# Order of side work around an attention pipeline: weight lengths a block later, tanh ahead of a projection, and a last head that evicts before it normalises

## The chip, the cores and the metric

The kernel runs on one core of a Trainium2 chip. The metric is the device time of one execution in microseconds; of several runs the median counts.

## The reference

Two branches share a layer-normalised input of 2048 rows and 640 columns. One is attention over a key and value cache with 32 heads of 192 columns and 2048 keys, the other a gated feed-forward net with 1536 hidden columns. Everything comes in as bf16.

```python
xn = _layernorm(x)                                   # (1, 2048, 640)
q = (xn @ wq).reshape(1, 2048, 32, 192).transpose(0, 2, 1, 3)
scores = einsum("bhqd,bhkd->bhqk", q, k_cache) * 192 ** -0.5
o = einsum("bhqk,bhkd->bhqd", softmax(scores), v_cache)
s = o.transpose(0, 2, 1, 3).reshape(1, 2048, 6144) @ wo
h = silu(xn @ w1) * (xn @ w3)
g = silu(h @ w2)
return x + s * g
```

## The kernel before

The attention part is a software pipeline over heads `h` (0 to 31), query blocks `qb` of 512 rows (0 to 3), and steps `p` (0 to 7), each with 256 keys. In a step TensorE makes scores of 256 keys by 512 queries (`scores`, line 550), ScalarE takes their exponential into a weight tile (`weights`, line 558), and one and a half steps or so behind TensorE multiplies earlier weights with the values into two PSUM banks `obank0` and `obank1` (`values_quads`, line 629; `values`, line 609). After step 7 of a block the banks are evicted while the next block starts: for heads 2 to 30 ("quads") ScalarE copies one bank to `oa` and DVE adds the other into `ot` (`evict_quads`, lines 653 and 654); for heads 0, 1 and 31 DVE makes `osum` of each bank and divides it by its row sum (`evict`, lines 581 to 588). There is one pair of value banks, so TensorE's first value product of a block waits for the eviction of the block ahead. The score banks, `ps_st`, are two; the weight tiles, pool `pp`, are three, each for two steps.

In step 1 of each block TensorE also projects a block of the next head's queries (`project_chunk`, line 355), and DVE, ScalarE and POOL copy the result into `qA`, `qF`, `qS` and `qD` (lines 378 to 385). In the last head that place holds the last columns of the feed-forward branch (`hidden_last`, results `gl` and `ul`, lines 950 and 951). In the projection's spare columns a part of the feed-forward branch is carried: every odd head takes `tanh` of the part that came with the head ahead of it (`gate`, line 524, ScalarE) and multiplies twice on DVE (`product`, lines 529 and 531).

For quads heads the row sums of the weights are made on DVE by a tree of additions (`row_sums`, line 662: twice a block the sum of four weight tiles, `fours`, then `join`, `fold`, `ends`, which leaves `e`), a DMA transpose of `e` into `eT`, and `turned_sums` (lines 702 to 709), which adds up, inverts and normalises the evicted outputs into `ostage`.

The exponentials need a bound for each head. It is made from the largest keys (`fold_keys`, three DVE reductions, line 407, and three small POOL copies into `sh`) and from the lengths of the weight columns (`column_lengths`): a DMA transpose of the head's weights into `wt`, issued on the SP queue (line 421), two DVE instructions that square and add (`squares`, line 428), and seven small ones for the root (`roots`, lines 434 to 442). `head_bound` puts the two together and adds over partitions on POOL (line 502).

Where side work stands is set by hand. Nearly everything is pinned to program order, engine by engine (`pin`). A counter `clock` goes up by one a step. `chores` hold work with a due time: `later(2, fours)`, `later(4, ...)` for the rest of the tree, `later(6, turned_sums)`; `do_chores` runs all that are due at the end of each step. `lazy` is a list of bound work that is taken one piece a step, from its head, in steps 5, 6 and 7 of even heads and of head 1, and in step 5 of other odd heads; a piece is taken only if its due time has come. In an even head the lengths of head `h + 1` are asked for in block 0, step 3, and those of `h + 2` in block 2. All engines work through their instructions in order, so an instruction that waits keeps everything behind it.

The tail, after head 31, makes the rest of the feed-forward branch and the output product; the change does not touch it.

Of the kernel before, what the change touches and what calls it, by code (L numbers as in the profile page):

```python
# [30 lines left out]
def _kernel_impl(ctx, tc, A_x, A_k_cache, A_v_cache, A_wq, A_wo, B_w1, B_w3, B_w2, out):  # L31
    nc = tc.nc
    _, SQ, D = A_x.shape
    _, H, SK, dh = A_k_cache.shape
# [131 lines left out]
    with ExitStack() as actx:  # L166
# [236 lines left out]
        def fold_keys(h):  # L403
            hd = heads[h]

            def piece(j):
                pin(nc.vector.tensor_reduce(out=hd["mk"][:, j:j + 1], in_=hd["L"]["KT"][:, j, :], axis=AX.X, op=ALU.max,
                                            apply_absolute_value=True))
                if j == 2:
                    sh, up, down = shift_tile()  # L410
                    up(hd["mk"])
                    down(hd["mk"])
                    hd["mk"] = (hd["mk"], sh)

            hd["mk"] = stt.tile([P, 3], F32, tag="mk", name="mk")
            return [(0, piece, (j,)) for j in range(3)]

        def column_lengths(h):
            L = loads.get(h) or heads[h]["L"]
            wt = fdp.tile([P, 2 * DC, P], BF16, tag="wt", name="wt")  # L420
            pin(nc.sync.dma_start_transpose(out=wt[:], in_=L["wq"][:].rearrange("p s c -> p (s c)")))
            ss = stt.tile([P, 2], F32, tag="ss", name="ss")
            pin(nc.vector.memset(ss[:], 0.0))

            def squares(t):
                r0 = (0, PGW)[t]
                v = wt[r0:P, :, ROWS[t]]
                pin(nc.vector.scalar_tensor_tensor(out=v, in0=v, scalar=1.0, in1=v, op0=ALU.mult, op1=ALU.mult,  # L428
                                                   accum_out=ss[r0:P, t:t + 1]))

            def roots():
                y = stt.tile([P, 2], F32, tag="ly", name="ly")
                z = stt.tile([P, 2], F32, tag="lz", name="lz")
                pin(nc.vector.tensor_scalar(out=ss[:], in0=ss[:], scalar1=float(D), scalar2=None, op0=ALU.mult))
                pin(nc.vector.tensor_scalar(out=y[:].bitcast(I32), in0=ss[:].bitcast(I32), scalar1=1, scalar2=None,
                                            op0=ALU.logical_shift_right))
                pin(nc.vector.tensor_scalar(out=y[:].bitcast(I32), in0=y[:].bitcast(I32), scalar1=0x1FC00000, scalar2=None, op0=ALU.add))
                pin(nc.vector.reciprocal(out=z[:], in_=y[:]))
                pin(nc.vector.tensor_tensor(out=z[:], in0=z[:], in1=ss[:], op=ALU.mult))
                ln = stt.tile([P, 2], F32, tag="ln", name="ln")  # L440
                pin(nc.vector.scalar_tensor_tensor(out=ln[:], in0=z[:], scalar=1.0, in1=y[:], op0=ALU.mult, op1=ALU.add))
                pin(nc.vector.tensor_scalar(out=ln[:], in0=ln[:], scalar1=0.5, scalar2=None, op0=ALU.mult))
                L["ln"] = ln

            return [(clock[0] + 4, squares, (0,)), (clock[0] + 4, squares, (1,)), (clock[0] + 4, roots, ())]

        def head_bound(h):
            hd = heads[h]
# [2 lines left out]
        def shift_tile():  # L451
            sh = stt.tile([P, 2], F32, tag="sh", name="sh")
            keep = pin if 0 in heads else (lambda x: x)
            keep(nc.gpsimd.memset(sh[ROWS[0], 1:2], 0.0))

            def up(m):
                keep(nc.gpsimd.tensor_copy(out=sh[ROWS[0], 0:1], in_=m[ROWS[1], 1:2]))

            def down(m):
                keep(nc.gpsimd.tensor_copy(out=sh[ROWS[1], 0:1], in_=m[ROWS[0], 2:3]))  # L460
                keep(nc.gpsimd.tensor_copy(out=sh[ROWS[1], 1:2], in_=m[ROWS[0], 1:2]))
            return sh, up, down
# [195 lines left out]
        def later(wait, f, *a):  # L658
            chores.append((clock[0] + wait, f, a))
# [55 lines left out]
        clock = [0]  # L715
        chores = []
        lazy = []
        aq = {}

        def do_chores(h, qb, p):  # L720
            for c in [c for c in chores if c[0] <= clock[0]]:
                chores.remove(c)
                c[1](*c[2])
            slots = (5, 6, 7) if h % 2 == 0 or h == 1 else (5,)
            if p in slots and lazy and lazy[0][0] <= clock[0]:
                _, f, a = lazy.pop(0)
                f(*a)
# [236 lines left out]
        for h in range(1, H):  # L964
            if h >= H // 2 and ffn_w_loads:
                ffn_w_loads.pop(0)()
            if h == 1:
                loads[3] = load_weights(3)
                while loads[2]["rest"]:
                    loads[2]["rest"].pop(0)()  # L970
            elif h + 2 == H:
                load_last()
            if h + 1 < H:
                start_head(h + 1)
            hd = heads[h]
            hd.update(sums=dict(w=[], t=[]), ox={})
            if h == 1:
                lengths = [2]
                todo = []
            elif h + 1 < H:  # L980
                lengths = [] if h % 2 else [h + 1] + [h + 2] * (h + 2 < H)
                todo = [h + 1]
            else:
                lengths = todo = []
            chunks = [[0], [1], [2], [3]] if h + 1 < H else [[0, 1], [2, 3], [], []]
            gated = []
            for qb in range(NQB):
                post = []
                if (h, qb) == (H - 1, 2):
                    while chores:  # L990
                        clock[0] += 1
                        do_chores(h, qb, 2)
                    astack.close()
                    acc["hTp"] = fstack.enter_context(tc.tile_pool(name="hTp", bufs=2, side="right"))

                def extra():
                    if h % 2 == 1:
                        for c in chunks[qb]:
                            gate = swiglu_chunk(h // 2, heads[h - 1]["qF"], hd["qF"], c)
                            gated.append(gate if h + 1 < H else gate())  # L1000
                    quads = before["quads"] if qb == 0 else hd["quads"]
                    if h + 1 < H:
                        post.append(project_chunk(h + 1, qb, quads=quads, cast_low=nc.scalar.copy if hd["quads"] else None))
                    else:
                        post.append(hidden_last(qb, quads))

                for p in range(NPAIR):
                    step(hd, qb, p, extra if p == 1 else None)
                    if p == 4 and 1 < h < H - 2:
                        load_ahead(h + 2, qb)  # L1010
                    if p == 3 and (h, qb) != (1, 0):
                        for k in lengths[:1] if qb % 2 == 0 or h == 1 else []:
                            lazy.extend(column_lengths(k))
                            lengths = lengths[1:]
                        for k in todo or ([2] if (h, qb) == (1, 1) else []):
                            lazy.extend(fold_keys(k))
                            lazy.append((0, head_bound, (k,)))
                        todo = []
                    if (h, qb, p) == (1, 0, 7):
                        copy_keys(heads[2]["L"])  # L1020
                        loads[3].update(load_keys(3))
                    if (h, qb, p) == (1, 2, 7):
                        copy_keys(loads[3])
                    if h + 1 < H:
                        if p == 3 and gated:
                            f = gated.pop(0)
                            later(1, lambda f=f: gated.append(f()))
                            later(3, lambda: gated.pop(0)())
                    else:
                        if p > 4 and gated:  # L1030
                            gated.pop(0)()
                        if p == 3:
                            gated.append(post.pop()())
            while lazy:
                _, f, a = lazy.pop(0)
                f(*a)
                assert 0, "late"
            heads.pop(h - 1, None)
            before["quads"] = hd["quads"]
# [143 lines left out]
    with ExitStack() as dctx:  # L1183
# [32 lines left out]
        todo = [lambda qb=qb, j=j: parts.append(load_part(pools, qb, j)) for qb in range(LB) for j in range(4)][3:]  # L1216
# [177 lines left out]
```

## Time and profile before

| | |
|---|---|
| median of 3 runs | 1941.54 us (1940.84 to 1942.04) |
| profiled execution | 1942.01 us |
| span of that execution on the core | 1940.5 us |
| TensorE matmul busy | 1919.0 us (99%) |
| DVE busy | 1440.0 us (74%) |
| ScalarE busy | 1351.7 us (70%) |
| granted TensorE clock | 1.0 of full speed |

Times in a timeline are microseconds from the span's start. A row of a timeline gives start, length, engine, line, operation, written and read tiles, and in brackets how long the engine was idle just before and what ended that. PE is TensorE, ACT is ScalarE, SP is the queue that issues most DMAs. A matmul's end is modelled, so the idle time of PE is best read together with the pitch at which the same instruction comes again in each block.

### The profile page before, as it was taken

What the parts mean: (1) busy time and instruction counts of PE and PEld (TensorE: products, weight loads), DVE (VectorE), ACT (ScalarE), POOL (GpSimd) and SP (SyncE); (2) the same over time, 40 slices, a digit from 0 to 9 for tenths busy, and PEclk for the clock granted to TensorE, in tenths of its full rate; (3) what the DMA queues carried; (4) which work ended last, traced back from release to release, by engine and by line L of the source; (5) the groups of instructions that cost most, each with busy time, mean ns of one, the idle gap of its engine ahead of it and who ended that gap; (6) DMA issues with size and microseconds to landing.
All of it is one profiled execution on the core that took longest, in us unless ns stands there. A gap on an engine that the chain in (4) does not pass through costs nothing.

```text
span 1940.5 us, 75768 instructions
## 1 busy us (share of the span) xinstructions
PE 1919.0 (99%) x34608; PEld 1550.9 (80%) x34631; DVE 1440.0 (74%) x2326; ACT 1351.7 (70%) x1405; POOL 602.9 (31%) x757
## 2 busy tenths in 40 slices
PE   9999999999999999999999999999999999999999
PEld 5666698999989998989898989888988986454446
DVE  8569897888888888888888979897988875521111
ACT  7778888788878788888788888888787877210000
POOL 3423334333434333334323343334343320000000
PEclk9999999999999999999999999999999999999999
DMA  7724446444553455445544454436444523946763
GB/s 169 138 53 74 104 84 101 86 99 86 92 97 84 99 81 98 81 103 91 103 84 102 68 107 72 113 73 106 84 99 88 97 42 111 276 84 144 165 148 79
DMA packets 535684, 197.22 MB, mean 102 GB/s; under 512 B 486896, under 2 KB 528848, under 8 KB 535360
## 3 DMA queue, kind: packets, MB, share of 16 engines
q1 hardware_dynamic: 522416, 162.71, 43.3%
q0 software_dynamic: 8256, 24.58, 5.1%
q8 instruction: 271, 4.44, 1.0%
q10 hardware_dynamic: 4688, 5.05, 0.8%
q14 instruction: 53, 0.43, 0.1%
HBM read 54.26 MB, written 31.98 MB: 44 GB/s over the span
## 4 chain that ended last, share of the span: by engine, by line
PE 88%; DVE 7%; DMA 3%; issue 1%; ACT 1%; SPq 0%; POOL 0%; DVEq 0%; ACTq 0%
PE st L550 30%; PE obank L629 28%; PE ps L355 13%; PE ps_s L1138 8%; DVE tree L662 3%; PE obank L609 3%; PE ps_s L1094 3%; DMA wt<-wq 3%; PE ps_f L1158 2%; PE ps_gu L927 1%; PE ps_f L1174 1%; DVE ot L654 1%; DVE wt L428 1%; DVE e L662 1%; DVE qA L378 0%
## 5 line engine op out<-in xcount | busy, mean ns | idle before, releaser
L558 ACT ACTIVATE pT<-st,nb 128x1024 bf16<-128x1024 f32 x1016 | 1125.9, 1114 | 197.2 <-PE st L550 170.0
L629 PE MATMUL obank<-pT,vt 64*64 64x512 bf16 (+1 forms) x14848 | 846.3, 323 | 11.4 <-DVE ot L654 11.3
L629 PEld LDWEIGHTS <-vt 64*64 64x64 bf16 x14848 | 604.1, 107 | 89.0 <-issue 20.0
L550 PE MATMUL st<-qS,KM 64*64 64x512 bf16 (+1 forms) x1951 | 469.9, 376 | 0.2 <-DVE ul L951 0.2
L550 PE MATMUL st<-qD,KT 64*64 64x512 bf16 (+1 forms) x1951 | 470.1, 376 | 0.0
L550 PE MATMUL st<-qA,KT 64*64 64x512 bf16 (+1 forms) x1951 | 470.0, 376 | 0.0
L550 PEld LDWEIGHTS <-KT 64*64 64x64 bf16 (+1 forms) x7808 | 379.6, 106 | 54.3 <-issue 0.6
L550 PE MATMUL st<-qA,KM 64*64 64x512 bf16 (+1 forms) x1951 | 413.9, 376 | 0.0
L550 PE MATMUL st<-qS,KT 64*64 64x512 bf16 (+1 forms) x1951 | 413.8, 376 | 0.1
L550 PE MATMUL st<-qF,KT 64*64 64x512 bf16 (+1 forms) x1951 | 413.8, 376 | 0.0
L381 POOL COPY qS<-qA 64x512 bf16<-64x512 bf16 x256 | 292.4, 1142 | 79.7 <-DVE qA L378 45.4
L662 DVE TENSOR_TENSOR tree<-pT,pT 128x2048 bf16<-128x2048 bf16 x232 | 300.7, 1296 | 2.0 <-ACT pT L558 2.0
L355 PE MATMUL ps<-xnT,wq 64*64 64x512 bf16 (+1 forms) x2390 | 298.2, 376 | 0.0
L355 PE MATMUL ps<-xnS,wq 64*64 64x512 bf16 (+1 forms) x2390 | 290.6, 376 | 0.0
L662 DVE TENSOR_TENSOR tree<-tree 128x2048 bf16<-128x2048 bf16 x232 | 261.8, 1129 | 4.0
L355 PEld LDWEIGHTS <-wq 64*64 64x64 bf16 (+1 forms) x4780 | 220.8, 107 | 30.5
L550 PEld LDWEIGHTS <-KM 64*64 64x64 bf16 (+1 forms) x3904 | 196.5, 106 | 31.1 <-issue 4.5
L385 POOL COPY qD<-qF 64x512 bf16<-64x512 bf16 x127 | 95.4, 751 | 366.3 <-ACT qF L378 362.4
L1138 PE MATMUL ps_s<-oT,wo_sb 128*128 128x512 bf16 x705 | 154.9, 379 | 0.8
L378 DVE CAST qA<-ps 128x512 bf16<-128x512 f32 x120 | 82.9, 691 | 80.0 <-ACT qF L378 79.4
L1138 PEld LDWEIGHTS <-wo_sb 128*128 128x128 bf16 x720 | 70.4, 98 | 84.9 <-issue 0.2
L653 ACT COPY oa<-obank 128x768 f32<-128x768 f32 x116 | 92.8, 800 | 62.6 <-PE obank L629 62.6
(159 smaller groups left out, 1669.8 us busy)
## 6 DMA issues: line engine op xcount, KB each, us to landing
o_scr<-ostage SPq DMA_DIRECT2D x64, 384.0 KB, 2.9
vt<-in_A_v_cache_dram SPq DMA_DIRECT2D x62, 384.0 KB, 5.0
wo_sb<-in_A_wo_dram POOLq DMA_DIRECT2D x1, 7680.0 KB, 30.5
wq<-in_A_wq_dram POOLq DMA_DIRECT2D x31, 160.0 KB, 4.1
hT_scr<-hblk SPq DMA_DIRECT2D x16, 256.0 KB, 2.9
xnS<-xnT POOLq DMA_DIRECT2D x8, 320.0 KB, 6.1
wq<-in_B_w_dram POOLq DMA_DIRECT2D x31, 80.0 KB, 3.7
wq<-in_A_wq_dram POOLq DMA_DIRECT2D x31, 80.0 KB, 3.3
```

What stands on the lines that cost most here:

```text
L355: pin(nc.tensor.matmul(halves[t][c, :], lhsT=w[ROWS[t], s, c], rhs=xs[ROWS[t], s // 2, qs], start=(s == 0), stop=(s == 2 * DC - 1)))
L378: pin(c(out=dst[:, qs], in_=src))
L381: keep(nc.gpsimd.tensor_copy(out=qS[ROWS[t], qs], in_=qA[ROWS[1 - t], qs]))
L385: keep(copy(out=qD[:, qs], in_=qF[PGW:P, qs]))
L550: pin(nc.tensor.matmul(st2[c, t * 512:(t + 1) * 512], lhsT=k[:, c], rhs=q[ROWS[t], qs], start=(s == 0), stop=(s == 2)))
L558: pin(nc.scalar.activation(out=pT2, in_=st2[:], func=ACT.Exp, scale=SCALE, bias=nb[:]))
L609: pin(nc.tensor.matmul(acc["o"][b][:, r, (j % 2) * 256:(j % 2) * 256 + DH + 1], lhsT=pT2[ROWS[r], t * 512 + j * P:t * 512 + (j + 1) * P], ...
L629: pin(nc.tensor.matmul(acc["o"][r][ROWS[c], int(low), 0:n], lhsT=vt[ROWS[r], t, p, c0:c0 + DT], rhs=pT2[ROWS[r], t * 512 + q0:t * 512 + q0 ...
L653: pin(nc.scalar.copy(out=oa[:], in_=banks[0]))
L662: pin(nc.vector.tensor_tensor(out=out, in0=a, in1=b, op=ALU.add))
L1094: pin(nc.tensor.matmul(ps, lhsT=oT[:, k, :], rhs=wo_sb[:, k, c0:c1], start=(k == 0), stop=(k == OC - 1)))
L1138: pin(nc.tensor.matmul(ps_of[d], lhsT=wo_sb[:, k, d * P:(d + 1) * P], rhs=part(k // KQ)[:, k % KQ, :], start=(k == 0), stop=(k == OC - 1)))
```

## The change

Three edits.

First, the pieces of `column_lengths` fall due ten steps after their DMA is issued instead of four, and in `lazy` the three key maxima of a head go ahead of the length pieces, with `head_bound` behind both. Block 0 of an even head then has the three maxima in steps 5 to 7, block 1 the two squares and the roots, block 2 the bound; before, block 0 had one square, block 1 a square, the roots and a maximum, block 2 two maxima and the bound. The lengths of `h + 2`, in block 3, keep their steps.

Second, in every odd head that is not a quads head (head 1; the last head did so already) the `tanh` is issued in step 1, ahead of the projection, instead of in step 4. The multiplications stay in step 6.

Third, in the last head `do_chores` returns at once in steps 0 and 1 of a block. What is left over from head 30 (the last `fours`, two `turned_sums`, and the end of the tree) is then issued in step 2, behind the evictions and behind the copies `gl` and `ul`.

```diff
@@ column_lengths
-            return [(clock[0] + 4, squares, (0,)), (clock[0] + 4, squares, (1,)), (clock[0] + 4, roots, ())]
+            return [(clock[0] + 10, f, a) for f, a in ((squares, (0,)), (squares, (1,)), (roots, ()))]
@@ do_chores
         def do_chores(h, qb, p):
+            if h == H - 1 and p < 2:
+                return
             for c in [c for c in chores if c[0] <= clock[0]]:
@@ extra, in step 1
                             gate = swiglu_chunk(h // 2, heads[h - 1]["qF"], hd["qF"], c)
-                            gated.append(gate if h + 1 < H else gate())
+                            gated.append(gate if hd["quads"] else gate())
@@ after step 3
                     if p == 3 and (h, qb) != (1, 0):
+                        keys = todo or ([2] if (h, qb) == (1, 1) else [])
+                        for k in keys:
+                            lazy.extend(fold_keys(k))
                         for k in lengths[:1] if qb % 2 == 0 or h == 1 else []:
                             lazy.extend(column_lengths(k))
                             lengths = lengths[1:]
-                        for k in todo or ([2] if (h, qb) == (1, 1) else []):
-                            lazy.extend(fold_keys(k))
+                        for k in keys:
                             lazy.append((0, head_bound, (k,)))
                         todo = []
...
                         if p == 3 and gated:
-                            f = gated.pop(0)
-                            later(1, lambda f=f: gated.append(f()))
+                            if hd["quads"]:
+                                later(1, lambda f=gated.pop(0): gated.append(f()))
                             later(3, lambda: gated.pop(0)())
```

## The prediction

> **What bounds the kernel now.** I read the page's busy table first, then who waits for whom on TensorE, then the chain that ended last in order of time, and last the timeline around each place that the change touches. The table has TensorE busy almost throughout, and the chain, too, is TensorE for 88% of the span:
>
> ```profile
> PE 88%; DVE 7%; DMA 3%; issue 1%; ACT 1%; SPq 0%; POOL 0%; DVEq 0%; ACTq 0%
> ```
>
> The 7% of DVE and 3% of DMA are the part that a reordering can reach. The waits (engine, its instruction, what it waited for: total us, times, longest) show what TensorE itself was short of, and what stood before that:
>
> ```profile
> PE obank L629 <- DVE ot L654: 11.3, 14, 1.4
> PE obank L609 <- ACT pT L558: 1.4, 2, 1.3
> PE obank L609 <- DVE osum L582: 1.0, 1, 1.0
> DVE wt L428 <- DMA wt<-wq: 59.6, 16, 4.6
> ```
>
> So TensorE stands still 14 times for `ot`, DVE's eviction of the value banks, and once each for a weight tile of ScalarE and for a last-head eviction. Modelled matmul ends make such waits too small, so I take the loss from the pitch of the projection, which is issued once in every query block (chain, start and length in us):
>
> ```profile
> 228.23 2.19 PE ps L355 x40
> 254.18 2.16 PE ps L355 x39
> 266.72 2.16 PE ps L355 x40
> 329.41 2.18 PE ps L355 x40
> 355.90 2.16 PE ps L355 x39
> 1599.78 2.16 PE ps L355 x40
> ```
>
> An undisturbed block takes 266.72 - 254.18 = 12.54 us. The two blocks from 228.23 took 25.95, 0.87 more than twice that; the two from 329.41 took 26.49, 1.41 more. From 228.23 to 1599.78 lie 27 heads of four blocks, 108 blocks: 1371.55 us against 108 x 12.54 = 1354.3. All that queued heads lose there is 17.2 us.
>
> **Part 1, the weight lengths.** In each even head the transposed weights `wt` are asked for in block 0, and DVE squares them four steps later. This is such a place:
>
> ```profile
> 234.59 1.21 DVE L662 TENSOR_TENSOR tree<-pT,pT 128x2048 bf16<-128x2048 bf16 x1
> 239.50 0.83 DVE L428 SCALAR_TENSOR_TENSOR wt<-wt 128x640 bf16<-128x640 bf16 x1 [3.70 <-DMA wt<-wq]
> 240.25 0.08 DVE L428 DVE_READ_ACCUMULATOR wt<-wt 128x1 f32 x1
> 243.25 0.95 DVE L654 TENSOR_TENSOR ot<-oa,obank 128x768 bf16<-128x768 f32 x1
> 244.26 1.17 PE L629 MATMUL obank<-pT,vt 64*64 64x512 bf16 x24 [0.47 <-DVE ot L654]
> ```
>
> DVE is done with the tree at 235.80, sits 3.70 us for the DMA, and only then reaches the row sums, the normalising, the next tree and `ot`, which ends at 244.20; TensorE goes on at 244.26. Since the loss was 0.87, `ot` would have been in time up to about 244.20 - 0.87 = 243.33.
>
> After the change the three key maxima of `fold_keys` stand here, and the squares and roots come a block later, some 13 steps behind their DMA instead of 4. The DMA keeps its place on SP. The maxima read keys that were loaded a head earlier, so they start at 235.80. Their price, and a block in which two of them already stand in this position:
>
> ```profile
> L407 DVE TENSOR_REDUCE mk<-KT x90: 1202/1206/1215, 112.4 to 1583.3; 128x1 f32<-128x1024 bf16 x90
> 260.71 1.62 DVE L662 TENSOR_TENSOR tree<-pT,pT 128x2048 bf16<-128x2048 bf16 x1
> 262.25 2.33 DVE L407 TENSOR_REDUCE mk<-KT 128x1 f32<-128x1024 bf16 x2
> 265.32 0.68 DVE L702 TENSOR_REDUCE rs<-eT 128x4 f32<-128x512 bf16 x1
> 268.32 0.95 DVE L654 TENSOR_TENSOR ot<-oa,obank 128x768 bf16<-128x768 f32 x1
> ```
>
> Two take 2.33 (1.17 each, as starts overlap ends), so three take 3.50 to 3.62. What follows is the same chain as now: from the end of the squares' read-out, 240.33, to the end of `ot`, 244.20, it is 3.87 us (in the other block, 265.32 to 269.27, 3.95). So `ot` ends at 235.80 + 3.55 + 3.9 = 243.25, just inside 243.33. The second block checks it: `ot` ended at 269.27, 2.55 behind its projection at 266.72, and that block kept its pitch. Measured so, the new `ot` ends 243.25 - (228.23 + 12.54) = 2.48 behind. Block 0 thus fills the idle time with work that has to be done anyway, and the wait goes almost wholly; what is late next is nothing, by 0.1 us. If the estimate is off by 0.2 us, the 14 places keep up to 2.8 us.
>
> In block 1 DVE now has squares, squares, roots instead of squares, roots, maximum (less work by about a third of a microsecond); in block 2 only the head's bound instead of two maxima and the bound, which takes off the smaller losses; block 3 is as before. Head 1 gets the same exchange where DVE has idle time. On POOL the three small copies of `sh` move ahead, behind `qS` copies of block 0 and before those of block 1; queued behind them are the next block's `qD` and `qS`, which wait for casts that come later. The bound comes two steps earlier, with its reduction on POOL. I cost all of this at nothing.
>
> Bounds for part 1: between 11.3 (the named waits alone) and 17.2 (all the loss). Nearest to the pitch rows, less a microsecond for losses not tied to DVE and a trace of residual wait: **-16.0 us**.
>
> **Part 2, tanh in head 1.** In the last head `gate()` was already called at once, and stays so; what changes is head 1. There the first tanh brings a table load between two exponentials:
>
> ```profile
> 78.50 1.11 ACT L558 ACTIVATE pT<-st,nb 128x1024 bf16<-128x1024 f32 x1 [2.08 <-PE st L550]
> 82.60 1.28 ACT L524 ACT_TABLE_LOAD   x1
> 83.89 0.63 ACT L524 ACTIVATE pt<-qF 64x512 bf16<-64x512 bf16 x1
> 84.43 2.09 ACT L558 ACTIVATE pT<-st,nb 128x1024 bf16<-128x1024 f32 x2
> 85.58 0.51 PE L609 MATMUL obank<-vt,pT 64*128 64x193 bf16 x8 [1.25 <-ACT pT L558]
> 75.59 2.16 PE ps L355 x20
> 89.69 2.16 PE ps L355 x20
> 102.37 2.16 PE ps L355 x20
> ```
>
> Load and tanh hold ScalarE from 82.60 to 84.43, 1.83 us, and TensorE waits. That block took 14.10 us, the next 12.68: 1.42 lost. After the change the pair stands right behind the exponential of step 1, where ScalarE has 2.08 us of idle time while TensorE projects (row at 78.50). 1.83 fits with 0.25 over: **-1.4 us**. Its operand is the previous head's `qF`, long there. In the other blocks a tanh alone moves, with no loss at either place. The least that this part can bring is 0 (load and tanh hidden as badly as now).
>
> [...]
>
> **Part 3, the last head.** Its chores are now skipped in steps 0 and 1. This has two sides. In block 1, DVE normalises head 30's last block between the two evictions, and TensorE waits for the second:
>
> ```profile
> 1613.56 0.68 DVE L702 TENSOR_REDUCE rs<-eT 128x4 f32<-128x512 bf16 x1
> 1615.43 0.55 DVE L581 COPY osum<-obank 128x386 f32<-128x386 f32 x1
> 1616.63 1.01 PE L609 MATMUL obank<-vt,pT 64*128 64x193 bf16 x20 [1.02 <-DVE osum L582]
> 1626.87 2.16 PE ps L355 x20
> 1639.54 2.16 PE ps L355 x20
> ```
>
> The normalising takes 1615.43 - 1613.56 = 1.87 us and now goes behind the evictions. From 1599.78 to 1626.87 two blocks take 27.09, against 2 x 12.67: 1.75 lost, of which I give 1.5 to this place, as the wait and its refill.
>
> But block 0 has the same skip, and there it costs. Now:
>
> ```profile
> 1596.73 0.69 DVE L702 TENSOR_REDUCE rs<-eT 128x4 f32<-128x512 bf16 x1 [1.94 <-DMA eT<-e]
> 1598.60 1.22 DVE L662 TENSOR_TENSOR tree<-pT,pT 128x2048 bf16<-128x2048 bf16 x1
> 1602.59 0.68 DVE L951 CAST ul<-ps 128x512 bf16<-128x512 f32 x1
> 1603.18 1.94 DVE L662 TENSOR_TENSOR tree<-tree 128x2048 bf16<-128x2048 bf16 x2
> 1602.73 1.11 ACT L558 ACTIVATE pT<-st,nb 128x1024 bf16<-128x1024 f32 x1
> 1604.84 0.38 PE L550 MATMUL st<-qS,KM 64*128 64x512 bf16 x1
> ```
>
> The row sums, the normalising (head 30, block 2) and the tree of head 30's last four weight tiles stand ahead of `ot`, from 1596.73 to 1599.8. In the changed order all of them follow `ul`, the second cast of the projection. That tree reads the tile in the pool `pp` (three buffers) that the exponential of step 2 overwrites: in the built program that exponential waits for this very tree. It is added behind ul: 1603.18, plus 1598.60 - 1596.73 = 1.87 for sums and normalising, plus 1.2 for the tree: 1606.2, where the exponential starts now at 1602.73. Its 1.11 us later, at 1607.4, TensorE may overwrite the scores bank for step 4, which it does now at 1604.84. **Loss 2.5 us**, all on TensorE; ScalarE behind it has room (a block of 12.67 with a projection of 2.16 leaves 1.3 us a step, an exponential takes 1.11), so it isn't lost twice. Bounds: 0, if the moved work ran in DVE's idle time ahead of `ot`, which the order excludes, and 3.5, the whole delay of the exponential. Part 3 together: -1.5 + 2.5 = **+1.0 us**. On SP the store of the block's outputs goes ahead of two loads of hidden rows; no wait of TensorE for those loads is among its waits, so nothing.
>
> **Sum.** -16.0 - 1.4 + 1.0 = -16.4 us. The profiled execution took 1942.01 (span 1940.5 and 1.5 around it), 0.47 over the median of the three runs, 1941.54. Taken off the median: **1925.2 us**; span of a profiled run about 1924.
>
> **The rivals.**
> A: the waits go, last head pays (forecast): 1925.2, chance 0.77.
> B: the maxima come just too late. The same tree operation took 1.21 us at 234.59 but 1.62 at 260.71, so DVE rows do stretch, and the reserve is 0.1. If block 0 is 0.25 to 0.4 us late in 14 heads, 3.5 to 5.6 us stay: 1929 to 1931. Against: 90 maxima all took 1202 to 1215 ns, and two of them behind the long tree at 260.71 still left `ot` in time. Chance 0.15.
> [...] Chance 0.02. [...]
> D, slower: three maxima in a row replace the DMA as the thing that holds `ot`. Today the mean loss is about 15 / 14 = 1.07 us a place. Parts 2 and 3 sum to -0.4, so the run is over 0.2% slower only if each place loses 0.31 more than today: `ot` 1.4 us past its limit, a maximum of 1.65 us instead of 1.2. At 1.8 us each: 14 x 0.8 - 0.4 = +10.8, 1952. Nothing in 90 samples comes near. Chance 0.03.
> E: the change doesn't do what it says: DVE meets another wait at the same place (the turned sums `eT` land late, as in the row at 1596.73 with 1.94 us of it), the loss stays: 1941. Against: `e` stands ahead of the tree at 234.59 and is used behind the maxima, at 239.3, over 4 us later. Chance 0.03.
>
> **How the numbers follow.** The range takes A with its unknowns: -17.2, -1.5 and no net cost in the last head give 1923.0 at the low end; residual waits of B with the low half of part 1 give 1930.0 at the high end. 0.2%, 3.9 us, is about what a measurement of this kernel tells from no change. Faster by more: A, B, C, 0.94; within: 0.03; slower: 0.03.
>
> **What would show it.** In the changed profile `wt<-wq` is no longer waited for in even heads, three L407 rows stand behind the tree, `ot` ends about 2.5 us after the projection's start, and blocks keep 12.54; head 1's first block takes 12.7 with its table load ahead of the exponential of step 2; ScalarE in head 31, block 0, waits about 3.4 us on DVE's tree and TensorE about 2.5, and the 1.02 wait in block 1 is gone. Wrong is the forecast if TensorE still waits for `ot` in even heads, or if a new releaser stands there.

## The result and the profile after

The changed kernel takes 1926.34 us (median of 4 runs, 1925.48 to 1927.09), the kernel before 1941.79 us (4 runs, 1940.84 to 1942.74) in the same comparison: ratio 0.992, 95% interval 0.9903 to 0.9937. The profiled execution of the changed kernel has a span of 1924.3 us, against 1940.5. The forecast was 1925.2, range 1923.0 to 1930.0.

What TensorE waited for after the change (waits: total us, times, longest), and then the shares of the chain that ended last:

```profile
PE obank L609 <- ACT pT L558: 3.1, 2, 2.9
PE fill L217 <- DVE cols L182: 1.9, 1, 1.9
PE st L550 <- POOL qS L381: 0.4, 1, 0.4
...
```

```profile
PE 99%; SPq 0%; DVE 0%; ACT 0%; DMA 0%; POOL 0%; issue 0%; ACTq 0%
```

The 14 waits for `ot` are gone, as is the wait for `wt` on DVE, and the chain that held 7% DVE and 3% DMA is TensorE alone. Head 1's wait of 1.25 us for a weight tile of ScalarE is gone, and a new one of the same kind stands in the last head: 2.9 us. The pitch of the projection at the place that the prediction worked out (chain of waits, start and length):

```profile
226.57 2.16 PE ps L355 x40
239.11 2.16 PE ps L355 x40
251.65 2.16 PE ps L355 x40
264.36 2.16 PE ps L355 x40
```

226.57 to 239.11 to 251.65 is 12.54 twice, where before two blocks lost 0.87. Over the 108 blocks up to the last head the excess over 12.54 fell from 17.1 to 0.8 us (measured at the first matmul of each projection). What is left stands in a few blocks such as the one from 251.65, 12.71 long; the profile names no releaser there, and most of these blocks differ in length from execution to execution. Why they are long stays open.

DVE at this place (timeline, block 0 of an even head):

```profile
232.92 1.21 DVE L662 TENSOR_TENSOR tree<-pT,pT 128x2048 bf16<-128x2048 bf16 x1
...
234.05 3.46 DVE L407 TENSOR_REDUCE mk<-KT 128x1 f32<-128x1024 bf16 x3
237.43 0.67 DVE L702 TENSOR_REDUCE rs<-eT 128x4 f32<-128x512 bf16 x1
...
240.43 0.94 DVE L654 TENSOR_TENSOR ot<-oa,obank 128x768 bf16<-128x768 f32 x1
```

The three maxima follow the tree without a gap and take 3.46 us; `ot` ends at 241.37, 2.26 us behind the projection's chain start at 239.11, where 2.48 was forecast.

### The profile page after: what moved, and what is told of

Same layout as the page of the kernel before. It is cut to its first block, busy times and chain, and to the rows that moved or that the text cites. A ratio compares the mean times of both kernels' runs of the same rounds, so it can differ in the third digit from the quotient of the medians.

```text
span 1924.3 us, 75788 instructions
## 1 busy us (share of the span) xinstructions
PE 1914.5 (99%) x34631; PEld 1306.8 (68%) x34631; DVE 1446.4 (75%) x2326; ACT 1350.4 (70%) x1405; POOL 600.3 (31%) x757
## 4 chain that ended last, share of the span: by engine, by line
PE 99%; SPq 0%; DVE 0%; ACT 0%; DMA 0%; POOL 0%; issue 0%; ACTq 0%
PE st L550 34%; PE obank L629 31%; PE ps L355 14%; PE ps_s L1142 8%; PE obank L609 3%; PE ps_s L1098 3%; PE ps_f L1162 2%; PE ps_gu L929 1%; PE ps_f L1178 1%; PE ps L340 0%; DMA KT<-in_A_k_cache_dram 0%; SPq L116 0%; PE ps_gu L340 0%; ACT pT L558 0%; SPq L100 0%; ACT xnT L283 0%
## 5 line engine op out<-in xcount | busy, mean ns | idle before, releaser
L629 PE MATMUL obank<-pT,vt 64*64 64x256 bf16 (+1 forms) x14848 | 787.8, 323 | 0.0
L629 PEld LDWEIGHTS <-vt 64*64 64x64 bf16 x14848 | 499.7, 107 | 172.4 <-issue 1.9
L550 PE MATMUL st<-qS,KM 64*64 64x512 bf16 (+1 forms) x1951 | 416.7, 376 | 0.4 <-POOL qS L381 0.4
L550 PE MATMUL st<-qA,KT 64*64 64x512 bf16 (+1 forms) x1951 | 416.6, 376 | 0.0
L550 PE MATMUL st<-qD,KT 64*64 64x512 bf16 (+1 forms) x1951 | 416.6, 376 | 0.0
L550 PE MATMUL st<-qF,KT 64*64 64x512 bf16 (+1 forms) x1951 | 391.8, 376 | 0.0
L550 PEld LDWEIGHTS <-KT 64*64 64x64 bf16 (+1 forms) x7808 | 286.6, 107 | 129.8 <-issue 0.6
L355 PEld LDWEIGHTS <-wq 64*64 64x64 bf16 (+1 forms) x4780 | 170.2, 107 | 74.7
L550 PEld LDWEIGHTS <-KM 64*64 64x64 bf16 (+1 forms) x3904 | 152.0, 106 | 54.8 <-issue 1.2
L654 DVE TENSOR_TENSOR ot<-oa,obank 128x768 bf16<-128x768 f32 x116 | 110.1, 949 | 36.2 <-ACT oa L653 35.8
```

Source lines behind the costliest of these rows:

```text
L355: pin(nc.tensor.matmul(halves[t][c, :], lhsT=w[ROWS[t], s, c], rhs=xs[ROWS[t], s // 2, qs], start=(s == 0), stop=(s == 2 * DC - 1)))
L550: pin(nc.tensor.matmul(st2[c, t * 512:(t + 1) * 512], lhsT=k[:, c], rhs=q[ROWS[t], qs], start=(s == 0), stop=(s == 2)))
L629: pin(nc.tensor.matmul(acc["o"][r][ROWS[c], int(low), 0:n], lhsT=vt[ROWS[r], t, p, c0:c0 + DT], rhs=pT2[ROWS[r], t * 512 + q0:t * 512 + q0 ...
L654: pin(nc.vector.tensor_tensor(out=ot[:], in0=oa[:], in1=banks[1], op=ALU.add))
```

## The experiments

### The three parts by themselves

Each edit was put alone on the kernel before, on one chip, where that kernel's median is 1939.85 us (21 runs). The cut of the changed kernel's third edit, used below, ran with them.

```diff
-            return [(clock[0] + 4, squares, (0,)), (clock[0] + 4, squares, (1,)), (clock[0] + 4, roots, ())]
+            return [(clock[0] + 10, f, a) for f, a in ((squares, (0,)), (squares, (1,)), (roots, ()))]
...
+                        for k in keys:
+                            lazy.extend(fold_keys(k))
                         for k in lengths[:1] if qb % 2 == 0 or h == 1 else []:
...
```

> Part 1 alone on the kernel before: lengths due ten steps behind their DMA, key maxima first. Theory (the three parts add up, and part 1 is the gain): the 108 blocks from head 4 on lose about 0.8 us instead of 17.2, so -16.4 us, about 1925.4 where the kernel before takes 1941.8; DVE no longer waits for wt; head 1's first block stays at 14.1 and the last head's first two blocks at 12.95 and 14.2. Rival (part of the gain needs the other two edits, for instance because a later head inherits a delay): less than 14 us.

Measured: 1924.95 us, ratio 0.9924 (0.991 to 0.9937), 14.9 us less. The 108 blocks lose 0.6 us, head 1's first block stays at 14.09, the last head's first two at 12.88 and 14.22. That is the theory's picture; the gain is 1.5 us less than expected because the kernel before loses less on this chip: the next two profiles, which keep its order in these blocks, lose 15.4 and 15.6 us there instead of 17.1. The loss went with DVE's wait for a DMA: the 14 blocks of the kernel before take from 13.24 to 14.20 us, the shortest where DVE waited 3.68 us for `wt`, the longest where it waited 4.56.

```diff
-                            gated.append(gate if h + 1 < H else gate())
+                            gated.append(gate if hd["quads"] else gate())
...
+                            if hd["quads"]:
+                                later(1, lambda f=gated.pop(0): gated.append(f()))
```

> Part 2 alone: tanh of head 1 ahead of the projection. Theory: head 1's first block 12.67 instead of 14.10, all else as before, -1.4 us, about 1940.4. Rival (the block's gain is lost again before head 2 begins, because the transition to head 2 is set by the bound): 1941.8.

Measured: 1938.57 us, 1.3 less, ratio 0.9992 (0.9983 to 1.0001): the interval touches no change, so the time alone doesn't show it. The profile does: head 1's first block takes 12.67 instead of 14.10, and the transition to head 2 gives nothing back.

```diff
         def do_chores(h, qb, p):
+            if h == H - 1 and p < 2:
+                return
```

> Part 3 alone: the last head's chores wait for step 2 in all its blocks. Theory (block 0 pays 3.05 us for the late tree, block 1 gains 1.55): +1.5 us, about 1943.3; ScalarE waits 3.7 us for the tree in block 0. Rival (the 3 us of block 0 come from the earlier arrival that part 1 brings, not from the skip): -1.5 us, 1940.3.

Measured: 1942.71 us, ratio 1.0013 (1.0004 to 1.0022), 2.9 slower. The rival falls: the third edit costs time without the other two. It costs more than expected, and the profile shows where. ScalarE waits for the tree exactly as in the changed kernel, and TensorE for ScalarE:

```profile
1603.08 1.22 DVE L662 TENSOR_TENSOR tree<-pT,pT 128x2048 bf16<-128x2048 bf16 x1
...
1604.41 2.12 ACT L558 ACTIVATE pT<-st,nb 128x1024 bf16<-128x1024 f32 x2 [3.73 <-DVE tree L662]
...
1605.58 0.51 PE L609 MATMUL obank<-vt,pT 64*128 64x193 bf16 x8 [2.88 <-ACT pT L558]
```

But the block takes 17.67 us, not 16.00. The rest is TensorE's granted clock. The windows (stretch; its length; busy time and instructions of PE, PEld, DVE, ACT, POOL; the granted clock; DMA share; GB/s) are cut at whole multiples of 3.413 us from the beginning of this clock's record, where it changed in these traces (last section); the first of each table holds most of the wait. First this kernel, then the changed one:

```profile
1603.40:1606.81 3.41, 1.23 (x20) 0.88 (x22) 3.31 (x5) 2.40 (x3) 0.00 (x0) 1.00 0.00 0
1606.81:1610.23 3.42, 3.42 (x40) 2.50 (x36) 2.99 (x6) 2.31 (x3) 0.00 (x0) 0.50 0.22 43
1610.23:1613.64 3.41, 3.41 (x56) 2.21 (x52) 0.00 (x0) 2.16 (x3) 0.00 (x0) 1.00 0.01 2
```

```profile
1587.63:1591.05 3.42, 1.47 (x26) 1.12 (x28) 3.32 (x5) 2.64 (x4) 0.00 (x0) 1.00 0.00 0
1591.05:1594.46 3.41, 3.41 (x60) 2.40 (x56) 2.74 (x6) 2.83 (x3) 0.00 (x0) 1.00 0.22 43
```

In the stretch behind the wait the granted clock is 0.50 in the one execution and 1.00 in the other, with 40 matmul records against 60. A stretch of 3.41 us at half the clock should cost about 1.7 us (an estimate from these rows); the two blocks differ by 1.67. Three of the eleven times of this kernel lie from 1941.28 to 1941.50, which is the expected +1.5 over 1939.85, and eight from 1942.37 to 1944.12; that fits a fall in most executions, but the times alone don't show it.

The three medians add up to -13.3 us, where the changed kernel as a whole gains 15.3 to 15.5 on other chips. If the third edit's median holds one such fall of the clock, the sum without it is -15.0.

### The third edit, cut in pieces

```diff
-            if h == H - 1 and p < 2:
+            if h == H - 1 and p < 2 and qb > 0:
```

> The changed kernel, with the last head's chores skipped in steps 0 and 1 only from its block 1 on. Theory: block 0 back to 12.95 from 16.0, block 1 stays 12.67, so 3.05 us less than the changed kernel: 1923.3, and 18.5 less than before. Rival (block 1 needs block 0's skip, since the sums of head 30 then stand earlier): block 1 back at 14.2, 1924.8.

Measured on the chip of the first three: 1922.24 us, ratio 0.9907 (0.9892 to 0.9923), 17.6 less than before. Block 0 of the last head is back at 12.89, block 1 stays at 12.67. The rival falls. This version beats both kernels (repeated below).

```diff
             for c in [c for c in chores if c[0] <= clock[0]]:
+                if h == H - 1 and p < 2 and c[1].__name__ != "turned_sums":
+                    continue
```

> The changed kernel, but in the last head's steps 0 and 1 the row sums and the normalising (turned sums) run as due and only the tree is skipped. Theory (the exponential of step 2 waits for the tree that reads its buffer, wherever DVE is by then): in block 0 the tree follows the cast ul directly, 1.87 us earlier than in the changed kernel, so block 0 about 14.1 instead of 16.0; block 1 has the normalising between its evictions again, 14.2 instead of 12.67. Total near 1926.0. Rival (the normalising in front of the tree is what block 0 pays for, not the tree): block 0 back to 12.95.

Measured: blocks 14.08 and 14.22, one run at 1925.51 us. Both as the theory has them. With the tree alone late, the block loses less by the 1.9 us that the normalising took ahead of it, and TensorE waits for the second eviction of block 1 again (1.0 us). So the tree's place sets block 0, and the normalising counts there only as far as it stands in front of the tree.

```diff
             if p % 2 == 0:
-                acc["w"] = pp.tile([P, 2, 1024], BF16, tag="pT2", name="pT2")
+                pool, tag = (aq["tree"], "tree") if acc.pop("alt", False) else (pp, "pT2")
+                acc["w"] = pool.tile([P, 2, 1024], BF16, tag=tag, name="pT2")
...
+            acc["alt"] = (hd["h"], qb, p) == (H - 1, 0, 2)
             pT2 = weights(st2, hd["nb"][qb], p)
```

> The changed kernel, but the weight tile of steps 2 and 3 of the last head's block 0 is taken from the tree's pool, so it overwrites nothing that the late tree still reads. Theory (the wait is for the buffer alone): ScalarE no longer waits for the tree, block 0 about 12.95 with the same order on every engine, 3.05 us less than the changed kernel, about 1923.3. Rival (DVE's late work holds TensorE by another way, the score bank that ul frees or the tree's own result): block 0 stays above 14.

Measured: block 0 takes 13.52, one run at 1922.67 us. The wait at step 2 is gone with every engine's order unchanged, so it was the buffer. The remaining 0.6 over 12.9 was not foreseen, and it is the same wait once more, one tile later (timeline of ScalarE):

```profile
1584.51 1.11 ACT L559 ACTIVATE pT<-st,nb 128x1024 bf16<-128x1024 f32 x1
1586.16 1.11 ACT L559 ACTIVATE pT<-st,nb 128x1024 bf16<-128x1024 f32 x1 [0.53 <-PE st L550]
1587.17 0.62 ACT L959 ACTIVATE t<-gl 128x512 bf16<-128x512 bf16 x1
1588.44 2.12 ACT L559 ACTIVATE pT<-st,nb 128x1024 bf16<-128x1024 f32 x2 [0.66 <-DVE tree L663]
```

With one tile taken from elsewhere, step 4 is the one that comes round to the buffer that the tree still reads, and it waits 0.66 us for it.

### Due time or order

```diff
-            return [(clock[0] + 10, f, a) for f, a in ((squares, (0,)), (squares, (1,)), (roots, ()))]
+            return [(clock[0] + 4, f, a) for f, a in ((squares, (0,)), (squares, (1,)), (roots, ()))]
```

> The changed kernel with the lengths due four steps behind their DMA as before, but the key maxima still first. Theory (a square four steps behind its DMA is what stalls DVE, in whichever block): the first lengths of a head, queued behind the maxima, come in block 1 all the same; the second ones, asked for in block 2, now stand in step 7 of block 2 and DVE waits for wt there. With only the bound ahead of them the wait is as long as before, 3.5 us, and ot is late by 0.7 to 1.4 us at 14 places: about +14 us against the changed kernel, 1940. Rival (the gain came from the order of the maxima alone, the due time does nothing): 1926.3.

Measured: 1950.96 us (one run; the kernel before 1940.30 on that chip). The waits:

```profile
PE obank L629 <- DVE ot L654: 19.7, 14, 2.2
...
DVE wt L428 <- DMA wt<-wq: 48.7, 14, 4.8
```

The theory's place is right: 14 waits for `wt`, now in block 2, and 14 late `ot`. Its size is too small: 25.6 us lost in the 108 blocks, some 15 expected. Of that, some 1.7 us (an estimate: 3.41 us at half the clock) are the granted clock, which fell to 0.50 for 3.41 us behind the longest of these waits (2.18 us; that block took 16.60). For the rest, DVE is later in block 2 before it even begins to wait (timeline of this kernel, block 2 of an even head):

```profile
972.50 2.64 DVE L662 TENSOR_TENSOR tree<-tree 128x2048 bf16<-128x2048 bf16 x2
...
975.83 1.61 DVE L662 TENSOR_TENSOR tree<-pT,pT 128x2048 bf16<-128x2048 bf16 x1
...
977.74 0.15 DVE L499 TENSOR_REDUCE ns<-pr 128x1 f32<-128x2 f32 x1
981.09 0.83 DVE L428 SCALAR_TENSOR_TENSOR wt<-wt 128x640 bf16<-128x640 bf16 x1 [3.19 <-DMA wt<-wq]
```

The tree takes 2.64 and 1.61 us here, 2.23 and 1.22 in block 0, and the transpose is issued behind it. In this block POOL copies keys and, behind them, `qD` and `qS` beside these additions; whether that slows the tree was not tried.

### One maximum more

```diff
             def piece(j):
+                if j == 0:
+                    pin(nc.vector.tensor_reduce(out=hd["mk"][:, 0:1], in_=hd["L"]["KT"][:, 0, :], axis=AX.X, op=ALU.max,
+                                                apply_absolute_value=True))
```

> The changed kernel with the first key maximum of each head done twice, one more DVE instruction of 1.17 us. Theory (in block 0 of an even head DVE has to be done with ot by 2.87 us behind the projection's start, and now is at about 2.46): ot at 3.63, 0.76 us lost at each of 14 places, +10.6 us, about 1936.9; odd heads, where ot ends at 2.0 and the maxima stand one to a block, lose nothing. Rival (DVE is not what sets these blocks once the DMA wait is gone): 1926.3.

Measured: 1939.65 us (one run), with 14 blocks of 13.36 to 13.44 us, 12.2 us lost in all, 0.87 at each place. At the first of them (timeline of this kernel; its block starts at the same time as in the changed kernel):

```profile
234.06 1.20 DVE L408 TENSOR_REDUCE mk<-KT 128x1 f32<-128x1024 bf16 x1
235.30 3.47 DVE L410 TENSOR_REDUCE mk<-KT 128x1 f32<-128x1024 bf16 x3
...
241.69 0.95 DVE L657 TENSOR_TENSOR ot<-oa,obank 128x768 bf16<-128x768 f32 x1
```

`ot` ends at 242.64 instead of 241.37, 1.27 us later, and the block loses 0.82. The rival falls: about 0.4 us was in reserve in block 0, and what the DVE instruction took beyond that was lost in full. The rest of the difference to the changed kernel is the last head, whose block 0 took 17.61 us; the granted clock was 0.50 for 3.41 us after the wait.

### The table load

```diff
+                        if (h, qb) == (1, 0):
+                            pin(nc.scalar.preload_act_table_set("exp_and_others"))
                         for c in chunks[qb]:
```

> The kernel before, with the load of ScalarE's table issued in step 1 of head 1's first block, tanh left in step 4. Theory (the load alone is what TensorE waits for; a tanh of 0.54 us in step 4 is hidden, as in the next three blocks): block 12.7 instead of 14.1. Rival (it is tanh's place that counts): about 13.2, or 14.1 if the load has to be made again at tanh.

Measured: head 1's first block 12.67 us, one run at 1939.41. ScalarE loads the table once, in the gap, and not again at tanh:

```profile
76.40 1.28 ACT L999 ACT_TABLE_LOAD   x1
78.47 1.11 ACT L558 ACTIVATE pT<-st,nb 128x1024 bf16<-128x1024 f32 x1 [0.79 <-PE st L550]
...
82.44 0.62 ACT L524 ACTIVATE pt<-qF 64x512 bf16<-64x512 bf16 x1
```

It is the load that mattered; a tanh in step 4 is hidden.

### Changed kernel and best version once more

> The changed kernel once more, beside the next one. Theory (its one wait of 2.9 us in the last head lets the granted clock fall afterwards in some executions and not in others, at 1.6 us each time): its times fall into two groups about 1.6 us apart. Rival (the clock depends on the kernel alone, and this one keeps it, as in its profile): one group.

> The version that skips the last head's chores only from block 1 on, again, on the same chip as the changed kernel. Theory: no wait of over 0.5 us is left in the last head, so one group of times within about 0.8 us, 3 us under the faster group of the changed kernel and 4.6 under its slower one. Rival (the wait was not what sets the groups): two groups here as well.

Measured on one chip, the kernel before at 1941.51 us (9 runs, 1940.66 to 1943.12): the changed kernel 1926.22 us, ratio 0.9924 (0.991 to 0.9937); the version that skips from block 1 on 1923.11 us, ratio 0.9905 (0.989 to 0.992). The first's times are 1926.06, 1926.14, 1926.22, 1927.49 and 1928.04, the second's 1922.19, 1922.98, 1923.24 and 1923.59. The expected 3 us between them is there. The two groups are not settled: the first's times could be read so, but the second, which has no such wait, spreads over 1.4 us itself, more than expected. That the clock falls in some executions rests on the profiles: after the 2.88 us wait it stayed at 1.00 in three of them (the changed kernel twice, and the one with the shorter due time) and fell in two (the third edit alone, and one maximum more). How the waits of these five lay is in the last section.

## Why the prediction was right

**What bounds.** The 14 stalls of TensorE behind one DMA wait of DVE were nearly the whole of the gain: the run with part 1 alone has it by itself. The chain's 7% and 3% were over-read as what a reordering can reach: 10% of 1940.5 us is 194, and 16 were to be had. The chain shows through which engines the work was followed back, not how much TensorE would gain; the pitch gave that, and the forecast rightly went by it.

**Part 1, -16.0.** Between the two profiles it is -16.3, between medians of the edit alone -14.9. That `ot` would be in time was right, but the reserve was mis-sized: 0.1 us was worked out, about 0.4 was there. Both of its sides were a little off. The chain's rows start up to 0.3 us behind a projection's first matmul. Measured at the first matmuls (228.06, 240.60 and 253.87), the block that the late `ot` of 244.20 disturbs loses 0.73 and not 0.87, so the limit is 243.47, 2.87 behind the projection; one maximum more gives 2.88. And `ot` ends 2.43 behind the first matmul, where 243.25 meant 2.65. Rival B, and D behind it, needed an overrun that did not come.

**Part 2, -1.4.** Block 14.10 to 12.67, and ScalarE shows why:

```profile
76.29 1.28 ACT L524 ACT_TABLE_LOAD   x1
77.58 0.63 ACT L524 ACTIVATE pt<-qF 64x512 bf16<-64x512 bf16 x1
78.35 1.11 ACT L558 ACTIVATE pT<-st,nb 128x1024 bf16<-128x1024 f32 x1
```

Load and tanh fit with 0.14 us over, and the load alone was what TensorE had waited for (the run with the table load moved by itself). Tanh starts 1.29 us behind the load's start, and the load 0.02 behind the end of the exponential ahead of it (76.27).

**Part 3, +1.0.** The mechanism was right, down to the instruction that waits; the term "Loss 2.5 us" was mis-sized. Measured are 16.00 - 12.95 = 3.05 for block 0 and 14.22 - 12.67 = 1.55 gained in block 1, together +1.5. In the changed kernel:

```profile
1587.08 1.22 DVE L662 TENSOR_TENSOR tree<-pT,pT 128x2048 bf16<-128x2048 bf16 x1
1588.41 2.12 ACT L558 ACTIVATE pT<-st,nb 128x1024 bf16<-128x1024 f32 x2 [3.73 <-DVE tree L662]
1589.58 0.51 PE L609 MATMUL obank<-vt,pT 64*128 64x193 bf16 x8 [2.88 <-ACT pT L558]
1589.92 0.38 PE L550 MATMUL st<-qS,KM 64*128 64x512 bf16 x1
```

The exponential starts at 1588.41, right behind the tree, as worked out. But ahead of the scores of step 4 that the working named, TensorE has eight value products to do that read that exponential's result, and it is held there. The scores start 0.34 us behind them. The rest is that the exponential itself starts a little later in the block than worked out. The working also took TensorE's clock as constant through a wait of this length; where it fell, block 0 took 17.67 and 17.61 us, 1.6 to 1.7 more. In the profiled execution of the changed kernel it did not fall (last section).

The sum of the block terms is -16.3 - 1.4 + 1.5 = -16.2, which is the difference of the two spans; the medians differ by 15.45. They fall short of the forecast -16.4 by about one: part 1 brings less where the kernel before loses less, and part 3 cost half a microsecond more. (1941.54 - 16.4 is 1925.1, not 1925.2; nothing hangs on it.)

## What to carry to other kernels

Put work whose data are already there into the gap ahead of an instruction that waits for a DMA, and move that instruction back by more than the DMA's flight (here 3.3 to 5.6 us from issue to landing, 30 transfers); it cost nothing here as long as the engine met the next deadline, which can be read from the pitch of a repeated instruction rather than from idle times. When a reader of a rotating buffer is moved later, look for the writer that comes round to this buffer: here moving one tree addition behind two casts cost 3 us in the last head, more than the edit brought elsewhere. Cutting an edit down to the blocks where it helps was worth another 3 us.

## What the runs showed of the hardware

In these traces the granted clock of TensorE changed at times that lie whole multiples of 3.413 us behind the beginning of its record. With the third edit alone the record begins at 5.96 us, the clock falls at 1606.81 and is back at 1610.23, which is 469 and 470 such stretches later. In the kernel before the record begins at 7.04 us, in the changed kernel at 7.26; there the clock goes from 1.00 to 0.50 at 1938.98 and 1922.13, behind the last matmul, 566 and 561 stretches later.

In these traces, what a long wait cost went with how it lay over the stretches. Five executions have the 2.88 us wait of the last head. Where one stretch holds 2.18 us or more of it (the third edit alone, with TensorE busy for 1.23 us of the stretch, and one maximum more, with 0.64), the granted clock is 0.50 throughout the next. Where the wait is split so that no stretch is idle for more than 1.95 us (TensorE busy for 1.47 us in the changed kernel, 1.83 and 2.11 in its repeat, 1.53 with the shorter due time), it stays at 1.00. With the shorter due time TensorE also waits 2.18 us for `ot`, all of it in one stretch, and the clock falls in the next:

```profile
573.14:576.55 3.41, 1.23 (x29) 0.72 (x25) 3.41 (x6) 1.46 (x2) 0.81 (x2) 1.00 0.32 78
576.55:579.97 3.42, 3.42 (x44) 2.31 (x40) 2.66 (x4) 1.11 (x1) 3.30 (x4) 0.50 0.31 58
```

Up to the stretch with the last matmul, these three are the only ones of the thirteen traces that are idle for more than 1.95 us, and the only ones with a fall behind them (idle time by modelled matmul ends). In the last head a fall cost 1.6 to 1.7 us (17.67 and 17.61 for block 0, against 16.00). The stretches with the last matmul, with a fall behind them as well, are idle for 2.35 us in the kernel before and 1.98 in the changed one. The 14 waits of the kernel before, named with at most 1.4 us, left blocks that lost up to 1.66 us, no stretch idle for more than 1.26 us before the last, and no fall there.
